# First batch of a softmax-weighted convolution before a max-out layer: softmax in two halves, half of the halo masked on GpSimd, and seven taps summed on TensorE for columns 8 to 11

## The chip, the cores and the metric

The kernel runs on one core of one Trainium2 chip. The metric is the device time of the slowest core (here the only one) in microseconds, as the median of several executions. The engines are TensorE (PE, with its weight load PEld), VectorE (DVE), ScalarE (ACT), GpSimd (POOL) and SyncE (SP, which here only issues transfers). An execution with the hardware profiler gives the trace from which all views below are taken.

## The reference, cut to what matters

```python
# x: [8, 4160, 192], weight_gen: [8, 4160, 8 heads, 7 taps], w1, w2: [192, 1024], w_out: [1024, 192]
w = exp(weight_gen - max over taps);  w = w / (sum over taps + 1e-9)
x_pad = six rows of zeros in front of each of the 8 sequences
y[b, s, h, g] = sum over k of w[b, s, h, k] * x_pad[b, s + k, h, g]      # 8 heads of 24 values
x1 = y.reshape(33280, 192)
out = maximum(x1 @ w1, x1 @ w2) @ w_out
```

A causal convolution with seven taps, whose weights are a softmax of their own for each row and head, is followed by a max-out layer.

## The kernel before

The 33280 rows are laid out as 128 partitions with 260 rows ("columns") each. Sixteen partitions hold one sequence, so the first partition of each sixteen needs six zero rows ahead of its first row, and the other partitions need the last six rows of their neighbour: this is the halo, which is loaded as `xs[:, 0:6*192]` and multiplied by a mask of 0 or 1. The columns are worked in batches of 16 (the last has 4). For a batch, `exp_sum` (ACT), `red` (DVE), `ln` (ACT) and `shift` (DVE) turn the raw weights into log-softmax values, `weights` (ACT) writes the exponentials doubled in bf16, `mul` (DVE) multiplies seven shifted copies of x with them, and `adds` (DVE) sums the taps.

```python
def exp_sum(b):
    e_ts[b] = pe_.tile([P, BATCHES[b][1] * WGC], FP32, name="e_t", tag="e")
    nc.scalar.activation(out=e_ts[b], in_=wg_ts[b], func=AF.Exp)

def red(b, i=0, of=1):
    ...
    nc.vector.reduce_sum(out=s_ts[b][:, hs], in_=_sub(e_ts[b], at, ap), axis=AX.X)

def ln(b):
    nc.scalar.activation(out=s_ts[b], in_=s_ts[b], func=AF.Ln)

def adds(b, o, first=False, beside=...):
    nc.vector.tensor_tensor(out=taps(0, 1, 3), in0=taps(0, 1, 3), in1=taps(3, 1, 3), op=ALU.add)
    if first:          # taps 3, 4, 5 are in taps 0, 1, 2 now; tap 6 is still alone
        return
    ...                # two more additions, the last into y_t
```

The first two batches are worked in pieces of four columns. For them `sum_transpose` adds the taps and transposes the result in one go on TensorE, by matrix products with an identity, and ACT copies the result to `yt`. With `LEFT` it reads four partial sums that a first addition on DVE has left, otherwise all seven taps. From batch 2 on DVE makes all three additions, and a transposing DMA gives `yt`.

```python
LEFT = (0, 1, 2, K - 1)

def sum_transpose(u, taps=range(K)):
    ...
    for k in range(6):
        for t in taps:
            for r in range(2):
                nc.tensor.matmul(yps[...], lhsT=m_t[half(r), at:at + P], rhs=ident[half(r), half(r)], ...)
    nc.scalar.copy(out=_sub(yt, ...), in_=_sub(yps, ...))
```

The maximum is taken as `x1 @ w1 + relu(x1 @ (w2 - w1))`: `wd` is `w2 - w1`, `hidden` multiplies `yt` with it on TensorE (two tiles for each group at first, three later) and applies the relu on ACT into `rd_t`, and `w10` is `w1 @ w_out`. `keep_warm` multiplies an identity with nothing to do. The engines work through their instructions in the order of the program text. The start of that text:

```python
load_wg(0, nc.sync)                      # weights of batch 0: one transfer
...                                      # halo, first four columns of x, first halves of w1 and w2
load_first(4)                            # columns 4 to 7 of x, into xs
...
exp_sum(0)
red(0)
ln(0)
shift(0)
nc.scalar.activation(out=xb_ts[0][:, 0:PAD * D], in_=xs[:, 0:PAD * D], func=AF.Copy, scale=msk[:, 0:1])
for o in (0, 4, 8, 12):
    weights(0, o)                        # two instructions each
nc.vector.tensor_copy(out=xb_ts[0][:, PAD * D:(PAD + 4) * D], in_=xs[:, PAD * D:(PAD + 4) * D])
mul(0, 0)
...
nc.scalar.copy(out=w1["E"][:, 0:HF], in_=ws["E", 0][:, 0:HF])
nc.scalar.copy(out=xb_ts[0][:, (PAD + 4) * D:(PAD + 8) * D], in_=xs[:, (PAD + 4) * D:])
...
nc.gpsimd.tensor_copy(out=gate[0:64, :], in_=ws["T", 1][:, 0:1])   # holds back GpSimd's own loads
load_x(0, 8, 4)
...
keep_warm(30)
w_diff(0, nc.scalar.copy)                # two subtractions on DVE, three copies on ACT
sum_transpose(0)
keep_warm(6)
mul(0, 4)
nc.scalar.copy(out=w1["E"][:, HF:F], in_=ws["E", 0][:, HF:F])
hidden(0)
nc.scalar.copy(out=w1["T"], in_=ws["T", 0])
w_diff(1, nc.vector.tensor_copy)
mul(0, 8)
sum_transpose(1)
exp_sum(1)
red(1)
adds(0, 8, True)
hidden(1)
ln(1)
shift(1)
mul(0, 12)
tp = w1_transposed()
hidden(2)
...
weights(1, 0)
mul(1, 0)
adds(1, 0, True)
sum_transpose(2, LEFT)
...
```

Of the kernel before, what the change touches and what calls it, by code (L numbers as in the profile page):

```python
# [9 lines left out]
FP32 = mybir.dt.float32  # L10
BF16 = mybir.dt.bfloat16
I32 = mybir.dt.int32
AF = mybir.ActivationFunctionType
ALU = mybir.AluOpType
# [3 lines left out]
def _sub(base: bass.AP, off: int, dims):  # L18
    ap = [list(base.ap[0])] + [[int(s), int(c)] for s, c in dims]
    return dataclasses.replace(base, offset=base.offset + off, ap=ap)  # L20
# [3 lines left out]
def kernel(  # L24
# [9 lines left out]
    nc = tc.nc  # L34

    B, S, D = x.shape
    H, K = weight_gen.shape[2], weight_gen.shape[3]
    F = moe_w1.shape[1]
    P = 128
    PAD = K - 1  # L40
    WGC = H * K
    FCH = F // P
    CPP = B * S // P
# [5 lines left out]
    BATCHES = [(c, min(16, CPP - c)) for c in range(0, CPP, 16)]  # L49
# [3 lines left out]
    def pieces(b):  # L53
        n = BATCHES[b][1]
        at, done = [], 0
        for w in (4, 4, 4, 4) if b < 2 else (8, 8) if n == 16 else (n,):
            at.append((done, w))
            done += w
        return at
# [17 lines left out]
    pe_ = ctx.enter_context(tc.tile_pool(name="pe", bufs=2))  # L77
# [20 lines left out]
    wg_ts, xb_ts, e_ts, s_ts, en_ts, y_ts, yt_ts = {}, {}, {}, {}, {}, {}, {}  # L98

    m_t = pm.tile([P, K * 16 * D], BF16, name="m_t")  # L100

    def load_wg(b, eng):
        c0, n = BATCHES[b]
        wg_ts[b] = pwg.tile([P, n * WGC], FP32, name="wg_t", tag="wg")
        eng.dma_start(
            out=wg_ts[b],
            in_=bass.AP(tensor=weight_gen.tensor, offset=c0 * WGC,
                        ap=[[CPP * WGC, P], [1, n * WGC]]),
        )

    def load_x(b, o, n):

# [9 lines left out]
                                in_=xb_ts[b - 1][:, 16 * D:(16 + PAD) * D])  # L122


    def exp_sum(b):
        e_ts[b] = pe_.tile([P, BATCHES[b][1] * WGC], FP32, name="e_t", tag="e")
        nc.scalar.activation(out=e_ts[b], in_=wg_ts[b], func=AF.Exp)  # L127

    def part(b, i, of):

        n = BATCHES[b][1]
        h0, h1 = n * i // of * H, n * (i + 1) // of * H
        return slice(h0, h1), h0 * K, [[K, h1 - h0], [1, K]]

    def red(b, i=0, of=1):
        if i == 0:
            s_ts[b] = psm.tile([P, BATCHES[b][1] * H], FP32, name="sum_t", tag="sum")
        hs, at, ap = part(b, i, of)
        nc.vector.reduce_sum(out=s_ts[b][:, hs], in_=_sub(e_ts[b], at, ap), axis=AX.X)  # L139

    def ln(b):
        nc.scalar.activation(out=s_ts[b], in_=s_ts[b], func=AF.Ln)  # L142

    def shift(b, i=0, of=1):
        hs, at, ap = part(b, i, of)
        w_t = _sub(wg_ts[b], at, ap)
        nc.vector.tensor_tensor(out=w_t, in0=w_t, in1=_sub(s_ts[b], hs.start, [[1, hs.stop - hs.start], [0, K]]),  # L147
                                op=ALU.subtract)
# [15 lines left out]
    def mul(b, o):  # L164

        n = dict(pieces(b))[o]
        if n == 4 and b < 2:
            m_out = _sub(m_t, K * o * D, [[64, 2], [P, K * 6], [1, 64]])
            x_in = _sub(xb_ts[b], o * D, [[2 * D, 2], [D, K], [1, 2 * D]])
        else:  # L170
            m_out = m_t[:, K * o * D:K * (o + n) * D]
            x_in = _sub(xb_ts[b], o * D, [[D, K], [1, n * D]])
        nc.vector.tensor_tensor(  # L173
            out=m_out, in0=x_in,
            in1=_sub(en_ts[b], o * WGC * 2, [[2, K * n * H], [0, G // 2], [1, 2]]),
            op=ALU.mult,
        )

    def adds(b, o, first=False, beside=lambda i, of: None):


        w = dict(pieces(b))[o]
        n = w * D

        def taps(at, step, cnt):
            return _sub(m_t, K * o * D + at * n, [[step * n, cnt], [1, w * D]])

        beside(0, 3)
        nc.vector.tensor_tensor(out=taps(0, 1, 3), in0=taps(0, 1, 3), in1=taps(3, 1, 3), op=ALU.add)  # L189
        if first:  # L190
            return
        beside(1, 3)
        if b not in y_ts:
            y_ts[b] = py.tile([P, 16 * D], BF16, name="y_t", tag="y")
        nc.vector.tensor_tensor(out=taps(0, 2, 2), in0=taps(0, 2, 2), in1=taps(1, 5, 2), op=ALU.add)  # L195
        beside(2, 3)

        nc.vector.tensor_tensor(  # L198
            out=_sub(y_ts[b], o * D, [[64, 2], [P, 3 * w // 2], [1, 64]]),
            in0=taps(0, 1, 1), in1=taps(2, 1, 1), op=ALU.add,  # L200
        )
# [22 lines left out]
    def half(j):  # L224
        return slice(64 * j, 64 * j + 64)


    LEFT = (0, 1, 2, K - 1)

    def sum_transpose(u, taps=range(K)):  # L230

        b, o, n = UNITS[u]
        assert n == 4
        yps = ps["r" if "r" in ps else "o"].tile([P, 1024], FP32, name="yps", tag="op")
# [3 lines that stand above are left out]
                    at = (K * o + t * n) * D + k * P  # L238
                    nc.tensor.matmul(
                        yps[:, r * 512 + k * 64:r * 512 + (k + 1) * 64],  # L240
                        lhsT=m_t[half(r), at:at + P], rhs=ident[half(r), half(r)],
                        start=(k == 0 and t == taps[0]), stop=(t == taps[-1]),
                        skip_group_check=True,
                    )
        yt = pyt.tile([P, 8 // 2 * 3 * P], BF16, name="yt", tag="yt")
        nc.scalar.copy(out=_sub(yt, 0, [[64, 2], [P, 6], [1, 64]]),  # L246
                       in_=_sub(yps, 0, [[512, 2], [64, 6], [1, 64]]))
        yt_ts[u] = yt
# [154 lines left out]
    for g in range(3, len(GROUPS)):  # L403
        most = 4 if g == 3 else 2 if GROUPS[g][1] == 2 or len(OUTS[-1]) == 4 else 4
        n = min(most, ready[g] - c)
# [78 lines left out]
    msk = consts.tile([P, 1], FP32, name="msk")  # L484
    gate = consts.tile([P, 1], FP32, name="gate")

    with tc.tile_pool(name="pstage", bufs=1) as pstage:
        ident_f = pstage.tile([P, P], FP32, name="ident_f")
        xs = pstage.tile([P, (PAD + 8) * D], FP32, name="xs")
        ws = {(kind, wi): pstage.tile([nr, F], FP32, name=f"ws{wi}{kind}")  # L490
              for kind, nr in (("E", P), ("T", 64)) for wi in range(2)}

        load_wg(0, nc.sync)
        nc.vector.memset(xs[0:1, 0:PAD * D], 0.0)
        for p0, p1, eng in ((16, P, nc.sync), (1, 16, nc.gpsimd)):
            eng.dma_start(
                out=xs[p0:p1, 0:PAD * D],
                in_=bass.AP(tensor=x.tensor, offset=(p0 * CPP - PAD) * D,
                            ap=[[CPP * D, p1 - p0], [1, PAD * D]]),
# [11 lines left out]
        def load_w(h):  # L511
            for kind, r0, nr in (("E", 0, P), ("T", P, 64)):
                for wi, wsrc in enumerate((moe_w1, moe_w2)):
# [14 lines left out]
        nc.vector.tensor_single_scalar(out=msk_i, in_=msk_i, scalar=1, op=ALU.min)  # L528
        nc.vector.tensor_copy(out=msk, in_=msk_i)
        nc.vector.tensor_copy(out=ident, in_=ident_f)  # L530
        exp_sum(0)
        red(0)
        ln(0)
        shift(0)
        xb_ts[0] = pxb.tile([P, (16 + PAD) * D], BF16, name="xb_t", tag="xb")
        nc.scalar.activation(out=xb_ts[0][:, 0:PAD * D], in_=xs[:, 0:PAD * D], func=AF.Copy,
                             scale=msk[:, 0:1])
        for o in (0, 4, 8, 12):
            weights(0, o)
        nc.vector.tensor_copy(out=xb_ts[0][:, PAD * D:(PAD + 4) * D],  # L540
                              in_=xs[:, PAD * D:(PAD + 4) * D])
        mul(0, 0)
        w1 = {kind: pstage.tile([nr, F], BF16, name="w1" + kind)
              for kind, nr in (("E", P), ("T", 64))}
# [3 lines left out]
        def w_diff(h, copy):  # L548

            c0, c1, c2 = (slice(s * F + h * HF, s * F + (h + 1) * HF) for s in range(3))  # L550
            nc.vector.tensor_tensor(out=wd[:, c0], in0=ws["E", 1][:, c0], in1=ws["E", 0][:, c0],
                                    op=ALU.subtract)
            copy(out=wd[64:P, c2], in_=wd[0:64, c0])
            copy(out=wd[0:64, c1], in_=wd[64:P, c0])
            nc.vector.tensor_tensor(out=wd[0:64, c2], in0=ws["T", 1][:, c0], in1=ws["T", 0][:, c0],
                                    op=ALU.subtract)
            copy(out=wd[64:P, c1], in_=wd[0:64, c2])
# [6 lines left out]
            out=wo[:, :].rearrange("p (f d) -> p f d", d=D),  # L564
            in_=bass.AP(tensor=moe_w_out.tensor, offset=0, ap=[[D, P], [P * D, FCH], [1, D]]),
# [23 lines left out]
        def keep_warm(times):  # L589

            for _ in range(times):
                nc.tensor.matmul(warm[:, 0:512], lhsT=ident, rhs=_sub(ident, 0, [[0, 4], [1, P]]),  # L592
                                 start=True, stop=True, skip_group_check=True)

        keep_warm(30)
        w_diff(0, nc.scalar.copy)
        sum_transpose(0)
        keep_warm(6)
        mul(0, 4)


        nc.scalar.copy(out=w1["E"][:, HF:F], in_=ws["E", 0][:, HF:F])
        hidden(0)
        nc.scalar.copy(out=w1["T"], in_=ws["T", 0])
        w_diff(1, nc.vector.tensor_copy)
        mul(0, 8)
        sum_transpose(1)
        exp_sum(1)
        red(1)
        adds(0, 8, True)  # L610
        hidden(1)
        ln(1)
        shift(1)
        mul(0, 12)
# [26 lines left out]
        weights(1, 0)  # L641
        mul(1, 0)
        adds(1, 0, True)
        sum_transpose(2, LEFT)
        load_x(2, 0, 16)
        load_wg(4, nc.gpsimd)
        rd = room(3)
# [138 lines left out]
```

The softmax here doesn't subtract the row's maximum and nothing guards it: scores larger than these inputs give would overflow.

## Time and profile before

| what | value |
|---|---|
| median of three runs | 413.91 us (413.67 to 413.95) |
| span of the profiled execution | 412.1 us |
| PE busy | 397.0 us, 96% |
| PEld busy | 316.0 us, 77% |
| DVE busy | 376.9 us, 91% |
| ACT busy | 359.2 us, 87% |
| POOL busy | 76.8 us, 19% |
| DMA | 65.68 MB, mean 159 GB/s |
| granted clock of TensorE | 0.997 |

A share of the span is an average over stages. The page also cuts the span into 40 equal slices of some 10.3 us each, with one digit of busy tenths for each engine, which shows the stages. The chain of waits follows the work that ended last back from the end, at each step to what released it. A timeline line gives the start in us, the duration in us, the engine, the line of the program, the operation and its operands, and in brackets how long the engine sat idle ahead of it and what ended that.

### The profile page before, as it was taken

How to read it: one execution, taken by the hardware profiler on the slowest of the kernel's cores; microseconds unless marked ns; L12 is line 12 of the kernel's file. 1: busy time of each engine (PE TensorE's matmuls, PEld its weight loads, DVE VectorE, ACT ScalarE, POOL GpSimd, SP SyncE). 2: the span in 40 equal slices, each digit the busy share in tenths (PEclk: the TensorE clock that was granted, in tenths of full speed). 3: DMA queues.
4: the chain of work that ended last, by engine and by line, in shares of the span. 5: the costliest groups of instructions: out<-in, count | busy, mean ns of one | idle time of the engine just before them, and what ended most of it. 6: DMA issues, size and time to landing. Idle time of an engine off the chain costs nothing.

```text
span 412.1 us, 15844 instructions
## 1 busy us (share of the span) xinstructions
PE 397.0 (96%) x7276; PEld 316.0 (77%) x7276; DVE 376.9 (91%) x218; ACT 359.2 (87%) x425; POOL 76.8 (19%) x102
## 2 busy tenths in 40 slices
PE   7879999999999999999999999999999999999994
PEld 2669899677777787777777777777777677777794
DVE  5999999999999999999999999999999999999000
ACT  5899998989999988999988999989998988888771
POOL 1510102212211212222012222220122221210000
PEclk9999999999999999999999999999999999999998
DMA  8975525775656875864896496578549747654613
GB/s 250 254 177 162 145 77 133 177 157 139 171 119 153 220 156 122 219 179 103 137 267 145 103 258 165 88 230 208 118 97 241 174 67 232 156 87 126 165 77 118
DMA packets 60242, 65.68 MB, mean 159 GB/s; under 512 B 47601, under 2 KB 48497, under 8 KB 60176
## 3 DMA queue, kind: packets, MB, share of 16 engines
q1 hardware_dynamic: 51904, 40.47, 35.4%
q0 software_dynamic: 8128, 24.11, 28.3%
q8 instruction: 57, 0.93, 0.9%
q10 hardware_dynamic: 144, 0.10, 0.1%
q14 instruction: 9, 0.07, 0.1%
HBM read 35.96 MB, written 25.56 MB: 149 GB/s over the span
## 4 chain that ended last, share of the span: by engine, by line
PE 44%; DVE 36%; ACT 12%; issue 3%; DMA 3%; SPq 1%; DVEq 0%; ACTq 0%
PE op_ps L315 21%; PE hd L275 19%; DVE m_t L173 18%; DVE m_t L189 8%; ACT rd_t L285 7%; DVE m_t L195 5%; PE op_ps L327 4%; DMA xs<-in_x_dram 2%; DVE y_t L198 2%; DVE sum_t L139 2%; DVE wg_t L147 1%; ACT en_t L158 1%; DMA yt<-y_t 1%; ACT yt L246 1%; PE hdp L275 1%
## 5 line engine op out<-in xcount | busy, mean ns | idle before, releaser
L285 ACT ACTIVATE rd_t<-hd 128x1024 bf16<-128x1024 f32 (+1 forms) x206 | 234.7, 1188 | 27.9 <-PE hd L275 26.4
L315 PE MATMUL op_ps<-wo,rd_t 64*128 64x192 bf16 x4160 | 210.5, 243 | 0.1
L315 PEld LDWEIGHTS <-rd_t 64*128 64x128 bf16 x4160 | 180.8, 94 | 15.7 <-ACTq L348 0.3
L275 PE MATMUL hd<-yt,wd 64*128 64x512 bf16 (+1 forms) x1584 | 187.5, 360 | 2.0 <-ACT rd_t L285 1.9
L173 DVE TENSOR_TENSOR m_t<-xb_t,en_t 128x10752 bf16<-128x10752 bf16 (+1 forms) x37 | 187.5, 5070 | 0.3 <-ACT en_t L158 0.3
L275 PEld LDWEIGHTS <-wd 64*128 64x128 bf16 x1776 | 94.0, 94 | 45.8 <-issue 4.9
L215 POOL CAST gate<-yt 128x1 f32<-128x1 bf16 x29 | 41.4, 1429 | 273.3 <-DMA yt<-y_t 273.3
L189 DVE TENSOR_TENSOR m_t<-m_t 128x4608 bf16<-128x4608 bf16 (+1 forms) x34 | 79.5, 2339 | 0.1
L371 ACT COPY o_t<-op_ps 128x384 f32<-128x384 f32 (+1 forms) x99 | 57.1, 588 | 13.7 <-PE op_ps L315 13.5
L327 PE MATMUL op_ps<-w,yt 64*128 64x192 bf16 x780 | 55.5, 243 | 1.7 <-ACT o_t L371 1.0
L327 PEld LDWEIGHTS <-yt 64*128 64x128 bf16 x780 | 38.4, 94 | 18.1 <-issue 2.6
L195 DVE TENSOR_TENSOR m_t<-m_t 128x3072 bf16<-128x3072 bf16 (+1 forms) x29 | 50.0, 1723 | 0.1
L158 ACT ACTIVATE en_t<-wg_t 128x896 bf16<-128x896 f32 (+2 forms) x45 | 35.3, 816 | 0.0
L198 DVE TENSOR_TENSOR y_t<-m_t 128x1536 bf16<-128x1536 bf16 (+1 forms) x29 | 27.3, 941 | 0.5
L361 DVE COPY o_t<-op_ps 128x192 f32<-128x192 f32 x1 | 0.4, 359 | 25.3 <-ACT o_t L361 25.3
L147 DVE TENSOR_TENSOR wg_t<-wg_t,sum_t 128x280 f32<-128x280 f32 (+4 forms) x45 | 22.0, 488 | 0.4 <-ACT sum_t L142 0.4
L139 DVE TENSOR_REDUCE sum_t<-e_t 128x64 f32<-128x448 f32 (+2 forms) x30 | 19.5, 650 | 2.5 <-ACT e_t L127 2.5
L115 POOL DMA_DIRECT2D xb_t<-in_x_dram x32 | 17.3, 540 | 23.1 <-DVE m_t L173 22.9
L127 ACT ACTIVATE e_t<-wg_t 128x896 f32<-128x896 f32 (+1 forms) x17 | 16.0, 939 | 2.5 <-DMA wg_t<-in_weight_gen_dram 2.5
L285 ACT ACTIVATE rd_t<-hdp 128x1024 bf16<-128x1024 f32 x16 | 15.9, 1027 | 1.0 <-PE hdp L275 1.0
L275 PE MATMUL hdp<-yt,wd 64*128 64x256 bf16 x192 | 13.0, 269 | 1.9 <-ACT rd_t L285 1.1
L592 PE MATMUL warm<-ident 128*128 128x512 bf16 x36 | 10.1, 445 | 3.0 <-DVE ident L530 3.0
(46 smaller groups left out, 74.4 us busy)
## 6 DMA issues: line engine op xcount, KB each, us to landing
out_dram<-o_t SPq DMA_DIRECT2D x28, 768.0 KB, 4.4
xb_t<-in_x_dram POOLq DMA_DIRECT2D x28, 384.0 KB, 4.8
wg_t<-in_weight_gen_dram POOLq DMA_DIRECT2D x14, 448.0 KB, 5.9
xb_t<-xb_t POOLq DMA_DIRECT2D x16, 288.0 KB, 5.0
out_dram<-o_t SPq DMA_DIRECT2D x8, 384.0 KB, 2.9
wg_t<-in_weight_gen_dram SPq DMA_DIRECT2D x2, 448.0 KB, 4.8
xs<-in_x_dram SPq DMA_DIRECT2D x2, 384.0 KB, 6.7
xb_t<-in_x_dram POOLq DMA_DIRECT2D x1, 768.0 KB, 6.9
```

The costliest lines, as they stand in the source:

```text
L139: nc.vector.reduce_sum(out=s_ts[b][:, hs], in_=_sub(e_ts[b], at, ap), axis=AX.X)
L158: nc.scalar.activation(out=_sub(en_ts[b], (o * WGC + j * N * K) * 2, [[2 * N, K], [2, N], [1, 2]]), in_=_sub(wg_ts[b], (o * H + j * N) * K ...
L173: nc.vector.tensor_tensor(out=m_out, in0=x_in, in1=_sub(en_ts[b], o * WGC * 2, [[2, K * n * H], [0, G // 2], [1, 2]]), op=ALU.mult,)
L189: nc.vector.tensor_tensor(out=taps(0, 1, 3), in0=taps(0, 1, 3), in1=taps(3, 1, 3), op=ALU.add)
L195: nc.vector.tensor_tensor(out=taps(0, 2, 2), in0=taps(0, 2, 2), in1=taps(1, 5, 2), op=ALU.add)
L198: nc.vector.tensor_tensor(out=_sub(y_ts[b], o * D, [[64, 2], [P, 3 * w // 2], [1, 64]]), in0=taps(0, 1, 1), in1=taps(2, 1, 1), op=ALU.add,)
L215: nc.gpsimd.tensor_copy(out=gate, in_=yt[:, 0:1])
L275: nc.tensor.matmul(hid_out(t, f, j), lhsT=wd[half(j), s * F + f * P:s * F + (f + 1) * P], rhs=_sub(yt_ts[u][half(j), :], (s + j) % 3 * P, ...
L285: nc.scalar.activation(out=rd[:, k * 1024:(k + n) * 1024], in_=hd[:, at:at + n * 1024], func=AF.Relu)
L315: return nc.tensor.matmul(op_out(c), lhsT=rd[half(r), k * 1024 + at:k * 1024 + at + P], rhs=wo[half(r), f * D:(f + 1) * D], start=False, s ...
L327: nc.tensor.matmul(op_out(c + j), lhsT=yt_ts[u][half(j), (3 * i + (s + j) % 3) * P:(3 * i + (s + j) % 3 + 1) * P], rhs=w10[half(j), s * D: ...
L371: nc.scalar.copy(out=_sub(o, c % 24 * D, [[D, len(qs)], [h * D, 2], [1, D]]), in_=_sub(tile_, at + (qs[0] - p) * D, [[D, len(qs)], [512, 2 ...
```

## The change

Three things are done, all in the first 30 us of the kernel. The softmax of batch 0 is split: its weights are loaded in two transfers of eight columns, and each of the four steps to the log-softmax becomes two instructions of half the size, so that ACT and DVE can work on different halves at one time. The first half of the halo (576 of 1152 values in each partition) is masked by GpSimd instead of ACT. For columns 8 to 11 of batch 0 the addition on DVE is taken away, and TensorE sums all seven taps. Along with this the idle products move (26 and 8 instead of 30 and 6), and the copy of the last 64 rows of w1 (`w1["T"]`) moves behind the copy of the second `yt` on ACT.

```diff
-    def load_wg(b, eng):
+    def load_wg(b, eng, of=1):
 ...
-        eng.dma_start(out=wg_ts[b], in_=..., ap=[[CPP * WGC, P], [1, n * WGC]])
+        w = n * WGC // of
+        for i in range(of):
+            eng.dma_start(out=wg_ts[b][:, i * w:(i + 1) * w], in_=..., ap=[[CPP * WGC, P], [1, w]])
 ...
-    def exp_sum(b):
-        e_ts[b] = pe_.tile([P, BATCHES[b][1] * WGC], FP32, name="e_t", tag="e")
-        nc.scalar.activation(out=e_ts[b], in_=wg_ts[b], func=AF.Exp)
+    def exp_sum(b, i=0, of=1):
+        if i == 0:
+            e_ts[b] = pe_.tile([P, BATCHES[b][1] * WGC], FP32, name="e_t", tag="e")
+        w = BATCHES[b][1] * WGC // of
+        nc.scalar.activation(out=e_ts[b][:, i * w:(i + 1) * w], in_=wg_ts[b][:, i * w:(i + 1) * w], func=AF.Exp)
 ...
-    def ln(b):
-        nc.scalar.activation(out=s_ts[b], in_=s_ts[b], func=AF.Ln)
+    def ln(b, i=0, of=1):
+        s_t = s_ts[b][:, part(b, i, of)[0]]
+        nc.scalar.activation(out=s_t, in_=s_t, func=AF.Ln)
 ...
-        load_wg(0, nc.sync)
+        load_wg(0, nc.sync, 2)
 ...
-        exp_sum(0)
-        red(0)
-        ln(0)
-        shift(0)
+        for step in (exp_sum, red, ln, shift):
+            for i in range(2):
+                step(0, i, 2)
         xb_ts[0] = pxb.tile([P, (16 + PAD) * D], BF16, name="xb_t", tag="xb")
-        nc.scalar.activation(out=xb_ts[0][:, 0:PAD * D], in_=xs[:, 0:PAD * D], func=AF.Copy,
+        HP = PAD * D // 2
+        nc.gpsimd.tensor_scalar(out=xb_ts[0][:, 0:HP], in0=xs[:, 0:HP], scalar1=msk[:, 0:1], scalar2=None,
+                                op0=ALU.mult)
+        nc.scalar.activation(out=xb_ts[0][:, HP:2 * HP], in_=xs[:, HP:2 * HP], func=AF.Copy,
                              scale=msk[:, 0:1])
 ...
-        keep_warm(30)
+        keep_warm(26)
         w_diff(0, nc.scalar.copy)
         sum_transpose(0)
-        keep_warm(6)
+        keep_warm(8)
 ...
-        nc.scalar.copy(out=w1["T"], in_=ws["T", 0])
         w_diff(1, nc.vector.tensor_copy)
         mul(0, 8)
         sum_transpose(1)
+        nc.scalar.copy(out=w1["T"], in_=ws["T", 0])
         exp_sum(1)
         red(1)
-        adds(0, 8, True)
         hidden(1)
 ...
-        sum_transpose(2, LEFT)
+        sum_transpose(2)
```

More of the change, by code (lines that the diff above doesn't have):

```diff
@@ L100 @@
     m_t = pm.tile([P, K * 16 * D], BF16, name="m_t")
-    def load_wg(b, eng):
+    def load_wg(b, eng, of=1):
         c0, n = BATCHES[b]
         wg_ts[b] = pwg.tile([P, n * WGC], FP32, name="wg_t", tag="wg")
[L105 to L109, printed above, removed]
+        w = n * WGC // of
+        for i in range(of):
+            eng.dma_start(
+                out=wg_ts[b][:, i * w:(i + 1) * w],
+                in_=bass.AP(tensor=weight_gen.tensor, offset=c0 * WGC + i * w,
+                            ap=[[CPP * WGC, P], [1, w]]),
+            )
     def load_x(b, o, n):
```

## The prediction

> **What bounds the kernel now.** I read the busy shares by slice first, then the chain of waits in order of time, then the timeline around every place where TensorE stood still, and last the first 25 us. The slices show that averages do not help: both PE and DVE are nearly full in every slice but the first and the last few.
>
> ```profile
> PE   7879999999999999999999999999999999999994
> ...
> DVE  5999999999999999999999999999999999999000
> ```
>
> DVE has no gap from slice 2 to slice 37 and then nothing to do; PE goes on for another 25 us. Which of them sets the pace is told by the chain of waits (start, duration, what):
>
> ```profile
> 136.04 1.32 PE op_ps L315 x32
> ...
> 144.67 1.32 PE op_ps L315 x32
> ...
> 212.46 5.75 DVE m_t L173
> ...
> 236.12 5.75 DVE m_t L173
> ...
> 342.83 4.00 DMA yt<-y_t
> 346.87 0.82 PE hd L275 x6
> ```
>
> Two rates can be read. PE repeats its pattern every 144.67 - 136.04 = 8.63 us for six columns, which is 23.02 us for a batch of 16. DVE repeats every 236.12 - 212.46 = 23.66 us. So DVE is slower by 0.64 us in each batch: it starts with a lead over PE and loses it. At 346.83 the last transfer of this chain (a transposed `y_t`) lands, and PE goes on with it at once; from there on PE alone sets the end. The timeline shows PE's weight load held until the very moment at which a `yt` lands, which the GpSimd copy `gate` marks:
>
> ```profile
> 311.09 0.33 PEld L275 LDWEIGHTS <-wd 64*128 64x128 bf16 x5 [0.20 <-issue]
> 311.17 1.75 POOL L215 CAST gate<-yt 128x1 f32<-128x1 bf16 x1 [9.10 <-DMA yt<-y_t]
> ...
> 323.54 1.01 PEld L275 LDWEIGHTS <-wd 64*128 64x128 bf16 x12 [1.00 <-PE op_ps L315]
> 323.55 1.18 POOL L215 CAST gate<-yt 128x1 f32<-128x1 bf16 x1 [9.63 <-DMA yt<-y_t]
> ...
> 346.87 0.33 PEld L275 LDWEIGHTS <-wd 64*128 64x128 bf16 x5 [0.43 <-issue]
> 346.95 1.44 POOL L215 CAST gate<-yt 128x1 f32<-128x1 bf16 x1 [9.37 <-DMA yt<-y_t]
> ```
>
> The idle names in the brackets mislead (no engine had just finished). The three stalls are 0.20 + 1.00 + 0.43 = about 1.6 us by the weight load, and about 1.4 us if I take PE's own gap of 0.81 at the second. This is all that DVE costs PE after 48 us. So the end is DVE's stream, through the `yt` of 346.83, plus PE's fixed rest. If DVE's stream moves earlier by d, the end moves by d, up to 1.4 us; there PE's own stream takes over.
>
> PE's own stream starts with ACT: from 11.70 to 31.5 us the chain is ACT almost without a break (it waits 0.40 us for PE at 16.18). The start:
>
> ```profile
> 11.70 0.83 ACT L547 CAST xb_t<-xs 128x768 bf16<-128x768 f32 x1 [0.63 <-DMA xs<-in_x_dram]
> ...
> 20.49 1.92 ACT L285 ACTIVATE rd_t<-hdp 128x1024 bf16<-128x1024 f32 x2
> 21.00 1.08 DVE L139 TENSOR_REDUCE sum_t<-e_t 128x128 f32<-128x896 f32 x1
> ...
> 22.00 1.35 DVE L189 TENSOR_TENSOR m_t<-m_t 128x2304 bf16<-128x2304 bf16 x1
> 22.30 0.31 ACT L142 ACTIVATE sum_t<-sum_t 128x128 f32<-128x128 f32 x1
> ...
> 23.27 1.08 DVE L147 TENSOR_TENSOR wg_t<-wg_t,sum_t 128x896 f32<-128x896 f32 x1
> ```
>
> ACT waits at 11.70 for columns 4 to 7 of x. Later, ACT's `ln` of batch 1 ends at 22.61, hidden behind DVE's addition at 22.00, the very one that the change removes.
>
> **What the Trainium skill says.** "SBUF — State Buffer", section "Who interferes with whom": a DVE instruction with two SBUF inputs or in a two-port mode and a GpSimd instruction that reads SBUF exclude one another for a whole instruction. The trace agrees: the GpSimd cast at 334.79, of one value per partition, takes 1.79 us and ends at 336.58, when DVE's product (330.79 + 5.75 = 336.54) ends. "GPSIMD Engine Reference", section "Elementwise — side-by-side cycle accounting": 1.8 cycles per element at 1.2 GHz in the best case; for 576 values that makes 0.86 us, an estimate, as no row here is such an operation. "DMA: Bandwidth & Descriptors", section "Queues, rings and completion order": on one DMA engine a ring is consumed in order. The trace fits: the x columns issued at 4.36 land only 7.32 us later, behind all that SyncE issued before them.
>
> **Part 1, the softmax in halves.** Before: exp 4.51 to 5.46, sum 5.50 to 6.58, ln to 6.92, subtraction to 8.05, then the exponentials from 8.08, because the mask (1.25 us) sits on ACT from 6.83; the product starts at 8.81. After: the DVE row for 128x448 takes 611 ns against 1081 for 128x896, so halving adds about 0.14 us per pair but overlaps. If the first half lands near 3.9 and the second near 4.6 (estimates from the landing at 4.51), the second exp ends near 5.2, the second sum near 5.8, the second ln near 6.1, and the subtractions near 7.1. But the halo lands at 1.27 + 5.5 = 6.8 and the first four columns of x at 1.66 + 6.0 = 7.7 (issue and time to landing of their transfers). DVE's cast of those columns then ends at 8.25, ACT's half mask (0.65 us, half of 1254 ns with its fixed part) at 7.45 and two exponentials near 8.1. The product could start at 8.3, 0.5 us earlier.
>
> **Part 2, the GpSimd mask.** It cannot start before the halo at 6.8 and finds the second subtraction holding the port until about 7.1; at 0.9 to 1.3 us it ends between 8.0 and 8.4. If it holds the port against the DVE cast at 7.7, the product starts at 8.6 to 9.0. So parts 1 and 2 together move it by between 0.5 us earlier and 0.2 us later.
>
> **Whether that is worth anything.** The next product needs ACT's cast of columns 4 to 7, which waits for the landing at 11.68 and ends at 12.53; it started at 12.89. So DVE can win at most 0.36 us here, and ACT nothing: its chain starts at 11.70 whatever happens before. The split makes 128 more packets. The queue view shows 188 packets of 0.68 MB at 95.1% of 16 engines from 3 to 5 us, or 162 ns for 3.6 KB, and 379 of 0.67 MB at 108.1% from 7 to 9 us, or 91 ns for 1.8 KB; a straight line leaves 23 ns for a packet, and 128 x 23 / 16 = 0.18 us. I call that **s**: the landing, and with it ACT's whole chain, slips by about 0.18 us.
>
> **Part 3, seven taps.** TensorE does 84 instead of 48 products there: before, 84 took 1.40 us and 48 took 0.87, so 0.53 us more. PE waits 0.39 us before them (until the addition ends) and 0.26 us later for ACT, so nothing reaches the chain. DVE loses one addition, 23.27 - 22.00 = 1.27 us. But `shift` then waits for `ln` of batch 1, which ends at 22.61 in ACT's own order, behind two relus. So `shift` starts at 22.65 + s instead of 23.27. The gain of DVE's stream is **d = 0.62 - s = 0.44 us**, whether or not part 1 won 0.36 us before: this wait swallows it. Moving the w1 copy behind the `yt` copy leaves ACT's sum as it was. After 23 us DVE waited for nothing; the exponentials that `mul(1, 0)` needs are ready at 26.41, and it would ask for them at 26.6 at the earliest, so d survives.
>
> **The sum.** 413.91 - 0.44 = 413.47 us, the end still set by DVE's stream.
>
> **Rivals.** (a) The naive sum: 1.27 us of addition and 0.36 us from part 1 move DVE by 1.6 us, PE takes over after 1.4 us, and the time is about 412.5. It needs an `ln` of batch 1 that is done by 21.9, and ACT's order speaks against that. (b) The start binds instead: the mask or the split holds ACT's or DVE's start back by 0.5 us or more; then d goes to zero, and PE's 1.4 us of slack hides the rest: 413.9 to 414.3. The 1.79 us cast is what speaks for it. (c) The landings decide: the transposes took 3.7 us as a rule but 4.3 at 319.17 and 4.0 at 342.83, when other transfers ran; shifted by half a microsecond they may meet others, 0.3 us either way.
>
> **Range and chances.** Point 413.45; (a) gives the lower end, 412.7, and (b) with (c) the upper, 414.2. Two per cent would be 8.3 us, while the whole stage in which the change works is 25 us with ACT full, so the chance of either side is about one in a hundred.
>
> **What would show it.** In the changed profile: DVE idle for 0.5 to 1.0 us before the subtraction of batch 1, released by ACT's `ln`; that subtraction near 22.7 to 22.9; the ACT cast of columns 4 to 7 near 11.9, still released by the DMA; the product of columns 0 to 3 between 8.3 and 9.0; the stalls at 311, 323 and 347 shrunk by about 0.4 us in sum, none gone everywhere. I am wrong if the subtraction starts before 22.3 (then rival a), if ACT's cast moves by more than 0.5 us (then the transfers were mis-sized), or if the chain no longer goes through DVE.

## The result, and the profile after

The changed kernel takes 416.50 us (median of 6 runs, 416.11 to 417.84), the kernel before 413.93 us (6 runs, 413.67 to 414.26). The ratio is 1.007 with a 95% interval of 1.0052 to 1.0088: within 2%, but slower, by about 2.6 us, and outside the predicted range.

The page of the changed kernel shows that another engine now sets the end. First three of the rows by slice, then the shares of the chain of waits by engine, after and before:

```profile
PE   7678899999999999999999999999999999999995
...
DVE  4989999999999999999999999999999999999100
...
PEclk9899999999999999999999999999999999999999
...
PE 83%; ACT 11%; issue 2%; DMA 2%; DVE 1%; POOL 0%; SPq 0%; POOLq 0%; DVEq 0%; ACTq 0%
```

```profile
PE 44%; DVE 36%; ACT 12%; issue 3%; DMA 3%; SPq 1%; DVEq 0%; ACTq 0%
```

DVE's third slice, which was full before, is at 8. PE's second, fourth and fifth slices have become emptier. The second slice of the granted clock has dropped below 9 tenths. The chain no longer goes through DVE (1%): it comes out of ACT (11%) and is then PE's own stream (83%). The timeline of the first 27 us shows why (SPq marks SyncE's issue of a transfer). First two lines of before, then after:

```profile
3.73 0.59 SPq L514 DMA_DIRECT2D ws1T<-in_moe_w_dram  x1
4.36 0.59 SPq L503 DMA_DIRECT2D xs<-in_x_dram  x1
```

```profile
3.33 1.12 ACT L131 ACTIVATE e_t<-wg_t 128x448 f32<-128x448 f32 x2 [1.33 <-DMA wg_t<-in_weight_gen_dram]
...
4.86 1.38 SPq L519 DMA_DIRECT2D ws1T<-in_moe_w_dram  x1
...
6.28 0.59 SPq L508 DMA_DIRECT2D xs<-in_x_dram  x1
...
8.87 0.78 ACT L543 ACTIVATE xb_t<-xs,msk 128x576 bf16<-128x576 f32 x1 [3.47 <-DMA xs<-in_x_dram]
8.99 1.99 POOL L541 TENSOR_SCALAR xb_t<-xs,msk 128x576 bf16<-128x576 f32 x1 [6.29 <-DMA xs<-in_x_dram]
...
11.01 2.96 DVE L178 TENSOR_TENSOR m_t<-xb_t,en_t 128x5376 bf16<-128x5376 bf16 x1 [0.55 <-POOL xb_t L541]
...
14.03 2.42 PE L244 MATMUL yps<-ident,m_t 64*128 64x64 bf16 x84 [3.46 <-DVE m_t L178]
...
14.61 0.83 ACT L554 CAST xb_t<-xs 128x768 bf16<-128x768 f32 x1 [2.10 <-DMA xs<-in_x_dram]
...
22.11 0.80 ACT L251 CAST yt<-yps 128x768 bf16<-128x768 f32 x1 [0.86 <-PE yps L244]
...
26.74 1.09 DVE L152 TENSOR_TENSOR wg_t<-wg_t,sum_t 128x896 f32<-128x896 f32 x1 [0.93 <-ACT sum_t L147]
```

The weights do what they were meant to do: the first exponential starts at 3.33 instead of 4.51. But what SyncE loads behind them is late. The halo lets ACT's mask start at 8.87, after 3.47 us of waiting; the first columns of x come at 9.9 instead of some 7.7. Columns 4 to 7 are issued at 6.28 instead of 4.36 and let ACT's cast start at 14.61 instead of 11.70. From there ACT's whole order of work is 2.9 us late. TensorE has run out of idle products and stands still for 3.46 us ahead of 14.03; its 84 products then take 2.42 us, where they took 1.40.

How the start becomes the end can be read from three lines of each kernel: the first `hidden` group of TensorE with the tiles of the steady state, TensorE's last products, and the last store that SyncE issues. First before, then after, then the version that loads the weights in one transfer (one_load below):

```profile
49.06 1.49 PE L275 MATMUL hd<-yt,wd 64*128 64x256 bf16 x24 [0.20 <-ACT rd_t L285]
...
404.56 2.16 PE L315 MATMUL op_ps<-wo,rd_t 64*128 64x192 bf16 x48
...
407.67 0.46 SPq L362 DMA_DIRECT2D out_dram<-o_t  x1
```

```profile
53.79 1.49 PE L280 MATMUL hd<-yt,wd 64*128 64x256 bf16 x24 [0.19 <-ACT rd_t L290]
...
408.16 2.16 PE L320 MATMUL op_ps<-wo,rd_t 64*128 64x192 bf16 x48
...
411.15 0.34 SPq L367 DMA_DIRECT2D out_dram<-o_t  x1
```

```profile
49.69 1.49 PE L280 MATMUL hd<-yt,wd 64*128 64x256 bf16 x24 [0.19 <-ACT rd_t L290]
...
404.02 2.16 PE L320 MATMUL op_ps<-wo,rd_t 64*128 64x192 bf16 x48
...
407.01 0.34 SPq L367 DMA_DIRECT2D out_dram<-o_t  x1
```

From the first of these lines to the end of TensorE's last product it is 357.7 us before, and 356.5 us in the two others: the stalls on DVE, 1.1 to 1.2 us, are gone. From that product to the end of the span it is 5.4 us before (412.1 - 406.7) and 4.5 us in the two others (414.8 - 410.3, 410.7 - 406.2): the last store leaves and lands 0.9 us sooner. So the changed kernel starts this stream 4.7 us later, saves 1.1 us of stalls and 0.9 us behind the last product, and ends 2.7 us later. The saving behind the last product stands in the traces of all seven versions that sum seven taps (4.5 to 4.6 us), and in none of those that keep the addition (4.8 to 5.8 us); why it goes with the seven taps was not found.

The 4.7 us are made up of four parts. ACT's cast of columns 4 to 7 is 2.9 us late. From the cast to the first relu ACT takes 0.2 us more (19.30 - 14.61 against 16.18 - 11.70), as the slow products and the eight idle products hold PE back. From that relu to the exponential of batch 1 it takes 1.0 us more, which is the wait of 0.86 us ahead of the second `yt` and what comes with it. The rest, 0.6 us, lies between that exponential and 53.79; one_load has it too (30.3 us against 29.4 before) and taps_only, with the seven taps alone, hardly (29.6), so it comes from another part of the change; which one was not isolated.

### The profile page after: what moved, and what is told of

It reads as the page before. It is cut to its first block, busy times and chain, and to the rows that moved or that the text cites. A ratio compares the mean times of both kernels' runs of the same rounds, so it can differ in the third digit from the quotient of the medians.

```text
span 414.8 us, 15920 instructions
## 1 busy us (share of the span) xinstructions
PE 398.0 (96%) x7310; PEld 317.5 (77%) x7310; DVE 376.1 (91%) x219; ACT 358.9 (87%) x427; POOL 81.4 (20%) x103
## 4 chain that ended last, share of the span: by engine, by line
PE 83%; ACT 11%; issue 2%; DMA 2%; DVE 1%; POOL 0%; SPq 0%; POOLq 0%; DVEq 0%; ACTq 0%
PE op_ps L320 38%; PE hd L280 36%; PE op_ps L332 7%; ACT rd_t L290 6%; DMA xs<-in_x_dram 2%; ACT en_t L163 1%; PE yps L244 1%; PE hdp L280 1%; ACT o_t L376 1%; DVE m_t L178 1%; ACT e_t L131 1%; PE warm L599 0%; POOL xb_t L541 0%; ACT yt L251 0%; ACT w1t L646 0%
## 5 line engine op out<-in xcount | busy, mean ns | idle before, releaser
L220 POOL CAST gate<-yt 128x1 f32<-128x1 bf16 x29 | 44.4, 1531 | 269.7 <-DMA yt<-y_t 269.7
L194 DVE TENSOR_TENSOR m_t<-m_t 128x4608 bf16<-128x4608 bf16 (+1 forms) x33 | 78.2, 2369 | 0.1
L376 ACT COPY o_t<-op_ps 128x384 f32<-128x384 f32 (+1 forms) x99 | 57.3, 592 | 13.5 <-PE op_ps L320 13.3
L152 DVE TENSOR_TENSOR wg_t<-wg_t,sum_t 128x280 f32<-128x280 f32 (+5 forms) x46 | 22.1, 481 | 0.9 <-ACT sum_t L147 0.9
L131 ACT ACTIVATE e_t<-wg_t 128x896 f32<-128x896 f32 (+2 forms) x18 | 16.1, 898 | 1.3 <-DMA wg_t<-in_weight_gen_dram 1.3
L244 PE MATMUL yps<-ident,m_t 64*128 64x64 bf16 x528 | 10.4, 198 | 4.2 <-DVE m_t L178 3.5
```

The source lines that it names most:

```text
L220: nc.gpsimd.tensor_copy(out=gate, in_=yt[:, 0:1])
L376: nc.scalar.copy(out=_sub(o, c % 24 * D, [[D, len(qs)], [h * D, 2], [1, D]]), in_=_sub(tile_, at + (qs[0] - p) * D, [[D, len(qs)], [512, 2 ...
```

## The experiments

My theory after the result was that the second weights transfer is the cause: it stands ahead of the halo and of x in SyncE's queue, and what follows is late. Rivals were the mask on GpSimd, the new order of ACT, the smaller packets of the split load, and an advantage of the addition that could be absent. Later two forms of the theory were to be told apart: that what follows is merely issued later, or that one more transfer in the queue costs by itself. The texts of expectation were written before each run and carry their own names for these. "Cast" is always ACT's cast of columns 4 to 7.

### The parts alone

**split_only**: the kernel before, with the weights of batch 0 loaded in two transfers and nothing else changed.

```diff
-    def load_wg(b, eng):
+    def load_wg(b, eng, of=1):
 ...
-        load_wg(0, nc.sync)
+        load_wg(0, nc.sync, 2)
```

> The kernel before with the load of batch 0's weights in two transfers, and nothing else changed. Theory A (the second transfer slows SyncE's whole stream of transfers; in the changed kernel columns 4 to 7 of x land at about 14.6 us instead of 11.7): the ACT cast of those columns starts near 14.6, DVE's stream is late by about 2.6 us and the time is 416.2 to 416.8 us. Theory B (the GpSimd mask, 1.99 us there, holds everything up): the cast stays near 11.9 and the time is 413.8 to 414.2 us. Theory C (the order of the w1T copy and the idle products cost it): 413.8 to 414.2 us as well.

Measured: 417.08 us (7 runs) against 413.95, ratio 1.0061 (1.0037 to 1.0086). Two lines of its timeline:

```profile
4.30 1.55 SPq L516 DMA_DIRECT2D ws1T<-in_moe_w_dram  x1
...
15.43 0.83 ACT L549 CAST xb_t<-xs 128x768 bf16<-128x768 f32 x1 [2.64 <-DMA xs<-in_x_dram]
```

The split alone makes the whole loss: the cast is at 15.43, and SyncE needs 1.55 us for an issue (`ws1T`) that took 0.59.

**one_load**: the changed kernel, with the weights in one transfer again; the softmax is still worked in halves.

```diff
-        load_wg(0, nc.sync, 2)
+        load_wg(0, nc.sync)
```

> The changed kernel with batch 0's weights in one transfer again; the four steps of the softmax stay in halves, the GpSimd mask, the seven taps and the orders stay. Theory A: the columns land near 11.7 us again and the time is 412.9 to 413.6 us, the gain of the removed addition. Theory B and C: still 415.5 us or more.

Measured: 413.07 us (20 runs), ratio 0.998 (0.9972 to 0.9988). It is faster than both kernels. Its timeline:

```profile
4.32 0.58 SPq L508 DMA_DIRECT2D xs<-in_x_dram  x1
...
11.08 0.83 ACT L554 CAST xb_t<-xs 128x768 bf16<-128x768 f32 x1 [0.78 <-DMA xs<-in_x_dram]
...
22.43 1.09 DVE L152 TENSOR_TENSOR wg_t<-wg_t,sum_t 128x896 f32<-128x896 f32 x1 [0.47 <-ACT sum_t L147]
```

One argument removes the loss. The cast is even earlier than before (11.08 against 11.70). DVE is no longer in the chain of waits (0%, PE 82%): with the stalls gone, TensorE's own stream sets the end.

**taps_only**: the kernel before, with part 3 alone.

```diff
-        adds(0, 8, True)
 ...
-        sum_transpose(2, LEFT)
+        sum_transpose(2)
```

> The kernel before with only the addition of columns 8 to 11 taken from DVE and all seven taps summed on TensorE. By the prediction's third part: batch 1's subtraction starts near 22.65 instead of 23.27 us, after a wait for ACT's ln, and the time is 413.2 to 413.4 us (0.6 us less). If the removed addition counted in full and the wait were absent, 412.5 to 412.8 us.

Measured: 413.15 us (9 runs), ratio 0.9976 (0.9963 to 0.9988). The line that the prediction was about:

```profile
22.37 1.09 DVE L147 TENSOR_TENSOR wg_t<-wg_t,sum_t 128x896 f32<-128x896 f32 x1 [0.40 <-ACT sum_t L142]
```

The subtraction of batch 1 starts at 22.37 instead of 23.27, and DVE waits 0.40 us for ACT's `ln`. As taps_only and one_load cannot be told apart, the halved softmax, GpSimd's mask, the moved idle products and the moved copy brought nothing that was measured: the whole gain goes with the seven taps. How much of it comes through DVE's stream is not shown, as 0.8 us of this trace's gain lie behind TensorE's last product (4.6 us to the end instead of 5.4).

**act_mask**: the changed kernel, with the whole halo masked by ACT.

```diff
-        nc.gpsimd.tensor_scalar(out=xb_ts[0][:, 0:HP], in0=xs[:, 0:HP], scalar1=msk[:, 0:1], ...)
-        nc.scalar.activation(out=xb_ts[0][:, HP:2 * HP], in_=xs[:, HP:2 * HP], func=AF.Copy,
+        nc.scalar.activation(out=xb_ts[0][:, 0:2 * HP], in_=xs[:, 0:2 * HP], func=AF.Copy,
                              scale=msk[:, 0:1])
```

> The changed kernel with the whole halo masked by ACT again, in one instruction. Theory A: the columns still land near 14.6 us and the time stays at 416.0 to 416.8 us. Theory B: the time falls to 413.0 to 413.8 us. Theory C: unchanged, 416 to 417 us.

Measured: 416.80 us (4 runs), ratio 1.0065 (1.004 to 1.0091); cast at 15.15. GpSimd's mask is slow, but it is not the cause.

### What of the second transfer costs

**act_queue**: the kernel before, with the second half of the weights issued by ACT at the same time, ahead of its table load.

```diff
-    nc.scalar.preload_act_table_set("natural_log_exp_and_others")
 ...
-        load_wg(0, nc.sync)
+        for h, eng in ((0, nc.sync), (1, nc.scalar)):
+            eng.dma_start(out=wg_ts[0][:, h * 8 * WGC:(h + 1) * 8 * WGC], in_=...)
+        nc.scalar.preload_act_table_set("natural_log_exp_and_others")
```

> The kernel before with batch 0's weights in two transfers of eight columns, the second issued by ACT ahead of its table load, so that SyncE issues the halo as early as before. Theory P: the packets are as small as in the changed kernel, the cast near 14 us, 416 us or more. Theory N: the cast at 11.4 to 12.0 us, 413.6 to 414.2 us.

Measured: 413.75 us (12 runs) against 413.88, ratio 0.9997 (0.9988 to 1.0005).

```profile
4.33 0.95 ACT L126 ACTIVATE e_t<-wg_t 128x896 f32<-128x896 f32 x1 [1.87 <-DMA wg_t<-in_weight_gen_dram]
...
11.14 0.83 ACT L553 CAST xb_t<-xs 128x768 bf16<-128x768 f32 x1 [0.25 <-DMA xs<-in_x_dram]
```

Two transfers are harmless if the second isn't in SyncE's queue. The Trainium skill says in "DMA: Bandwidth & Descriptors", section "Issuing engines are not separate DMA queues", that starting transfers from several engines saves only the issue time, as all run on the same 16 DMA engines. For the weights the trace agrees: they are complete no more than 0.2 us earlier (4.33 against 4.51). For what stands behind them the runs differ from it: the issue that SyncE saves is 0.46 us (the halo at 1.19, against 1.65 with both halves in its own queue in split_only), but the time differs by 0.64% (ratios 0.9997 and 1.0061), some 2.6 us.

**small_packets**: the kernel before, with one transfer of 256 packets of 1792 bytes. Columns 8 to 15 are computed with other weights than the reference's.

```diff
-        load_wg(0, nc.sync)
+        nc.sync.dma_start(out=_sub(wg_ts[0], 0, [[8 * WGC, 2], [1, 8 * WGC]]),
+            in_=bass.AP(..., ap=[[CPP * WGC, P], [16 * WGC, 2], [1, 8 * WGC]]))
```

> The kernel before with batch 0's weights in one transfer that reads two separate stretches of 1792 bytes for each partition (columns 0 to 7 and, instead of 8 to 15, 16 to 23; so columns 8 to 15 of the output are computed with other weights, with the same work): 256 packets of half the size, but one transfer. Theory P: the cast near 14.5 us, 416 to 417.5 us. Theory N: the cast at 11.4 to 12.0 us, 413.7 to 414.3 us.

Measured: 414.05 us (12 runs), ratio 1.0003 (0.9995 to 1.0012), cast at 11.08. The 128 more packets cost nothing.

**by_rows**: the kernel before, with two transfers of 64 partitions each; the packets keep their 3584 bytes.

```diff
-        load_wg(0, nc.sync)
+        wg_ts[0] = pwg.tile([P, 16 * WGC], FP32, name="wg_t", tag="wg")
+        for p0 in (0, 64):
+            nc.sync.dma_start(out=wg_ts[0][p0:p0 + 64, :], in_=...)
```

> The kernel before with batch 0's weights in two transfers on SyncE's queue, split by partitions (0 to 63, 64 to 127) and not by columns: 128 packets of 3584 bytes as before, but two transfers. Theory P (the packets of half the size do the harm): the cast of columns 4 to 7 on ACT starts at 11.4 to 11.9 us as before, 413.7 to 414.2 us. Theory N (one more transfer in SyncE's queue does it: it puts off the issue of the halo by 0.46 us, the transfer engines run dry and do not recover their rate): the cast near 14.5 to 15.5 us, 416 to 417.5 us.

Measured: 415.31 us (12 runs), ratio 1.0031 (1.0021 to 1.004); cast at 13.47. That lies between the two forecasts. So two transfers in one queue cost without small packets too, about half as much. Here the two issues alone take 1.21 us (0.87 with the split by columns).

**tiny_between**: the kernel before, with a transfer of one row of 224 bytes between the weights and the halo.

```diff
         load_wg(0, nc.sync)
+        tiny = pstage.tile([1, WGC], FP32, name="tiny")
+        nc.sync.dma_start(out=tiny, in_=...)
```

> The kernel before with one more transfer of a single row of 224 bytes (not used by anything) in SyncE's queue between the weights of batch 0 and the halo: the issue of the halo is put off by some 0.4 us and hardly a byte is added. Theory P: the cast at 11.4 to 12.1 us, 413.7 to 414.3 us. Theory N: the cast at 13.5 us or later, 415.5 to 417.5 us.

Measured: 414.75 us (20 runs, 412.93 to 417.54), ratio 1.0023 (1.0008 to 1.0037); cast at 12.55, again between the forecasts. A transfer that moves almost nothing costs 0.9 us (0.3 to 1.5 by the interval), and in the slowest executions 3 us and more.

**delay_only**: the kernel before; the halo's issue is made to wait for a small fill on DVE, with no transfer added.

```diff
+        hold = pstage.tile([1, 400], FP32, name="hold")
+        held_by = nc.vector.memset(hold, 0.0)
 ...
+            tc.add_manual_dep(halo.ins, held_by.ins.name, ...)   # SyncE's part of the halo
```

> The kernel before with the issue of the halo (and so of all that SyncE issues after it) put off until a small memset on DVE has ended, near 1.6 to 1.65 us instead of 1.19: as late as in the changed kernel, with no transfer more. Theory T (the later issue is what does the harm): the ACT cast of columns 4 to 7 at 13.5 us or later, 415.3 to 417.3 us. Theory X (one more transfer in the queue does it by itself): the cast at 11.4 to 12.2 us, 413.7 to 414.3 us.

Measured: 414.08 us (12 runs), ratio 1.0004 (0.9995 to 1.0012). The dose failed: the fill ended early, and the halo was issued at 1.30, only 0.11 us later than before (1.19). The run decides nothing.

**delay_half** and **delay_one**: the same with a longer fill and with a wait for the fill of `xs`; the halo is issued at 1.72 and at 2.08.

```diff
+        hold = pstage.tile([1, 800], FP32, name="hold")      # delay_half: twice the length
+        held_by = nc.vector.memset(hold, 0.0)
 ...
+        held_by = nc.vector.memset(xs[0:1, 0:PAD * D], 0.0)  # delay_one
```

> The kernel before with the issue of the halo put off until a memset of 800 values on DVE has ended, near 1.7 us instead of 1.19 (in the changed kernel 1.65); no transfer more. Theory T (the later issue does the harm): the ACT cast of columns 4 to 7 at 13.5 us or later, 415.3 to 417.3 us. Theory X (the additional transfer does it by itself): the cast at 11.4 to 12.2 us, 413.8 to 414.5 us.

> The kernel before with the issue of the halo put off until DVE's memset of the halo's first row has ended, near 2.1 us, 0.9 us later than before. Theory T: the cast at 14 us or later, 416 us or more. Theory X: every landing moves by at most the delay, the cast at 11.8 to 12.6 us, 413.8 to 415.0 us.

Measured: delay_half 415.18 us (19 runs, 413.76 to 418.27), ratio 1.003 (1.0014 to 1.0045); the profiled execution ran at a lower clock (424.14 us) and is left out, and of its trace only the time of the halo's issue is used. delay_one 414.96 us (7 runs), ratio 1.0022 (1.001 to 1.0034); cast at 12.27. A later issue alone costs 0.9 to 1.2 us, and the longer delay does not cost more. So in the median lateness is a part of the loss, but not the 2.6 us. The spread says more than the median: the kernel before stays within 413.14 and 414.94 us on the same chip, while delay_half reaches 417.5 to 418.3 us in three of its executions, as much as split_only. So a later issue alone can, in some executions, cost as much as the second transfer.

**tiny_first**: the kernel before, with the tiny transfer ahead of the weights.

```diff
+        tiny = pstage.tile([1, WGC], FP32, name="tiny")
+        nc.sync.dma_start(out=tiny, in_=...)
         load_wg(0, nc.sync)
```

> The kernel before with the additional transfer of one row of 224 bytes as the first of SyncE's queue, ahead of the weights. If the number of transfers counts: as with the tiny one behind the weights (cast 12.55, 414.75 us), 414.4 to 415.1 us. If it counts only between the weights and the halo: the cast at 11.4 to 12.2 us, 413.8 to 414.4 us.

Measured: 414.48 us (12 runs), ratio 1.0009 (1.0 to 1.0018); cast at 11.61, for which ACT did not wait. Everything is issued 0.4 us later, and it costs no more than that. The interval overlaps that of tiny_between (1.0008 to 1.0037), so that the place matters for so small a transfer is probable and not shown.

**after_late_half**: the changed kernel, with the second half of the weights on SyncE, but issued behind the halo.

```diff
-        load_wg(0, nc.sync, 2)
+        def load_half(h):
 ...
+        load_half(0)
 ...                                 # the halo
+        load_half(1)
```

> The changed kernel with both halves of the weights on SyncE's queue, but the second one issued behind the halo. If the harm comes from a second transfer of weights ahead of the halo: the cast at 11.2 to 12.3 us and 412.9 to 414.0 us. If any additional transfer of this size in this part of the queue does it: the cast at 13.5 us or later, 415.3 us or more.

Measured: 414.34 us (12 runs), ratio 1.0005 (0.9995 to 1.0015); cast at 12.62. By the ratios, each against the kernel before on the same chip, this is 0.25% above one_load; with the second half ahead of the halo it is 0.9% (1.007 against 0.998). So the transfer costs much less behind the halo, and is still not free: cast and time lie between the two forecasts.

What the runs have in common is easiest to see if the path to the cast is cut in two: when SyncE issues columns 4 to 7, and how long it is from there to the cast. All values are from the timelines, one execution each; only runs in which ACT really waited for the transfer are listed. The execution of after_w1t_first (below) is the slowest of its 20.

| kernel | issue, us | cast, us | issue to cast, us |
|---|---|---|---|
| before | 4.36 | 11.70 | 7.3 |
| taps_only | 4.37 | 11.37 | 7.0 |
| one_load | 4.32 | 11.08 | 6.8 |
| act_queue | 4.33 | 11.14 | 6.8 |
| small_packets | 4.46 | 11.08 | 6.6 |
| after_act_queue | 4.55 | 11.41 | 6.9 |
| tiny_between | 4.58 | 12.55 | 8.0 |
| after_late_half | 5.07 | 12.62 | 7.6 |
| delay_one | 5.28 | 12.27 | 7.0 |
| by_rows | 6.45 | 13.47 | 7.0 |
| split_only | 5.90 | 15.43 | 9.5 |
| act_mask | 5.88 | 15.15 | 9.3 |
| after_w1t_first | 5.54 | 15.67 | 10.1 |
| after | 6.28 | 14.61 | 8.3 |

The loss has two parts. In the changed kernel the issue is 1.9 us later: 0.47 us for the additional issue, and the rest because SyncE's two issues of `ws0T` and `ws1T` take 1.28 and 1.38 us instead of 0.56 and 0.59. And the way from the issue to the landing is about 1 us longer, in split_only 2.2; with one execution each, how much of that difference is chance is open. by_rows has only the first part, tiny_between almost only the second. The stretches of the trace show the second part as a rate: us, length, busy time of five engines, granted clock, DMA share, GB/s. First before, then after, then delay_one:

```profile
3.00:6.00 3.00, 2.99 (x8) 1.07 (x9) 0.51 (x1) 0.95 (x1) 0.00 (x0) 1.00 1.03 310
6.00:9.00 3.00, 3.00 (x13) 1.31 (x12) 2.33 (x4) 2.39 (x6) 0.00 (x0) 1.00 1.04 334
9.00:12.00 3.00, 2.77 (x25) 1.16 (x24) 3.00 (x2) 2.37 (x8) 1.01 (x2) 1.00 1.03 330
```

```profile
3.00:6.00 3.00, 2.98 (x8) 1.03 (x9) 2.06 (x4) 1.64 (x4) 0.00 (x0) 1.00 0.91 230
6.00:9.00 3.00, 3.00 (x14) 1.35 (x13) 0.18 (x1) 0.13 (x1) 0.01 (x1) 1.00 1.01 269
9.00:12.00 3.00, 1.57 (x8) 0.48 (x5) 1.55 (x2) 3.00 (x10) 1.98 (x1) 1.00 1.06 227
12.00:15.00 3.00, 0.97 (x38) 0.98 (x40) 3.00 (x3) 0.90 (x2) 1.52 (x3) 0.74 1.06 266
```

```profile
9.00:12.00 3.00, 3.00 (x15) 1.18 (x12) 2.70 (x2) 2.81 (x9) 0.47 (x1) 1.00 1.04 261
```

The DMA share adds up the times that packets took, over 16 engines. From 6 to 12 us it is 1.01 to 1.06 in both kernels, but after the change 269 and 227 GB/s are moved instead of 334 and 330, although the small packets of the weights have long landed. It is not a matter of larger or smaller packets either. From 9 to 12 us the trace has

```profile
DMA packets 480, 0.99 MB, mean 330 GB/s; under 512 B 55, under 2 KB 55, under 8 KB 480
```

before and

```profile
DMA packets 343, 0.68 MB, mean 227 GB/s; under 512 B 51, under 2 KB 51, under 8 KB 343
```

after: of the same mean size (2.1 and 2.0 KB), but a packet takes 149 ns instead of 103 (the share times 16 engines times 3 us, by the number of packets). Why a second transfer at 1.2 us makes packets slower until 12 us stays open. Packet size does not explain it (small_packets), and lateness explains at most a part: delay_one, with no transfer more, has 261 GB/s from 9 to 12 us.

### Two steps of the changed kernel on their own

**after_act_queue**: the changed kernel, with the second half of the weights issued by ACT.

```diff
-    nc.scalar.preload_act_table_set("natural_log_exp_and_others")
 ...
-        load_wg(0, nc.sync, 2)
+        for h, eng in ((0, nc.sync), (1, nc.scalar)):
+            eng.dma_start(out=wg_ts[0][:, h * 8 * WGC:(h + 1) * 8 * WGC], in_=...)
+        nc.scalar.preload_act_table_set("natural_log_exp_and_others")
```

> The changed kernel with the second half of batch 0's weights issued by ACT ahead of its table load, instead of by SyncE; all else of the change stays. If only the place of that transfer in SyncE's queue costs the time: the cast at 11.0 to 11.8 us, 412.8 to 413.5 us, like the changed kernel with one transfer (413.07). If a second transfer costs wherever it is issued: 415.5 us or more.

Measured: 413.41 us (14 runs) against 414.12, ratio 0.9986 (0.9977 to 0.9994); cast at 11.41. The loss is gone again, with two transfers and all of the rest in place. But ACT's first exponential starts at 4.29: on two queues the halves come together, so the softmax in halves has nothing to win.

**after_w1t_first**: the changed kernel, with the copy of `w1["T"]` at its old place ahead of the second `yt`.

```diff
         hidden(0)
+        nc.scalar.copy(out=w1["T"], in_=ws["T", 0])
 ...
         sum_transpose(1)
-        nc.scalar.copy(out=w1["T"], in_=ws["T", 0])
```

> The changed kernel with the copy of w1's last 64 rows on ACT ahead of the second yt copy again, as in the kernel before. In the changed kernel's trace ACT stood 0.86 us for TensorE's sums ahead of that yt copy, which this copy (1.04 us) would fill: 415.5 to 416.0 us. If the wait is not on the path: 416.3 to 416.7 us, as the changed kernel.

Measured: 415.75 us (20 runs, 414.34 to 418.48), ratio 1.0041 (1.0028 to 1.0055), against 1.007 (1.0052 to 1.0088) for the changed kernel. That fits with the 0.86 us of ACT's wait, which the copy would fill; but the intervals overlap a little and the executions spread over 4 us, so it is probable and not shown.

## Why the prediction was wrong

- **What bounds the kernel.** DVE's stream was in the chain of the kernel before (36%), and the stalls on it are 1.1 to 1.2 us, somewhat below the estimate of 1.4. That the end would be "still set by DVE's stream" held only in part, though: in taps_only DVE is still in the chain (31%), but in one_load, where the start stays in place, the stalls are gone, and PE's stream sets the end.
- **The step that failed: s.** The prediction gave the split 128 packets at 23 ns on 16 engines, 0.18 us, and concluded that ACT's chain "slips by about 0.18 us". It slipped by 2.9. The form of the term was wrong, not only its size: small_packets shows that the packets cost nothing, while the transfer, of which the sum had no term, costs the later issue and the lower rate of what follows. The landings of the halo (6.8) and of the first columns (7.7) were taken over from before as well; they came at 8.8 and 9.9.
- **Part 1.** The halves of the weights landed at 3.3 and by 3.9, 0.6 us and more ahead of the estimates (3.9 and 4.6). That was worth nothing, because the product then waited for the halo. The sentence that ACT's chain "starts at 11.70 whatever happens before" named the right instruction and the wrong reason for calm: it is a landing, and the change touches the queue that it is in.
- **Part 2.** GpSimd's mask took 1.99 us (1.73 to 1.86 in the other versions that have it) instead of 0.9 to 1.3. The estimate of 0.86 us from "GPSIMD Engine Reference", section "Elementwise — side-by-side cycle accounting", was a best case for another operation; the measurement decides. The mask released the first product (0.55 us of DVE's wait), as the prediction feared, and this is not what the end depends on (act_mask). That the mask would hold the port against DVE's cast was not seen: the cast ran from 9.90 to 10.46, inside the mask (8.99 to 10.98), and took 0.56 us against 0.55 before; in one_load it took 0.75.
- **Part 3.** Right for the start of the subtraction: it waits for ACT's `ln`, 0.40 us in taps_only and 0.47 in one_load, and starts at 22.37 and 22.43 instead of the 22.65 that the prediction gave without s. In taps_only ACT's first relu was 0.26 us earlier than before (15.92 against 16.18), as the columns had landed earlier; without that, the 0.90 us are 0.64, and 0.62 were forecast. That the time fell by 0.80 us (0.5 to 1.5 by the interval) fits, but in part by luck: the 0.8 us behind the last product were in no term of the sum.
- **The moved copy.** "Leaves ACT's sum as it was" holds only while ACT finds its work ready. In the late start it waits 0.86 us for PE, and the copy that could have filled this comes after.
- **The rivals.** (b), a late start that takes over, was the right one and was made too small: 0.5 us from the mask or the split, covered by PE's slack. With 4.7 us it was beyond any slack. Two of the three signs named for being wrong were met: the cast moved by more than 0.5 us, and the chain left DVE.
- **Not foreseen.** The idle products ended at 10.57, with the sums ready only at 14.03. The Trainium skill, "TensorE: Matmul & The Clock Gate", section "Part 1: The HAM clock gate", has the clock go down to half after an idle window of about 3.4 us. The trace agrees only in part. The clock does fall to half, for some 3 us, and the 84 products take 1 us more, but it falls at about 13.5 us, 2.9 us after the last idle product; in split_only it falls at 14.5 us, with only 2.05 us without products ahead of the 84 products, which had begun by then (after, then split_only; in the lines of stretches the clock stands third from the end):

```profile
13.50:14.00 0.50, 0.00 (x0) 0.00 (x0) 0.50 (x2) 0.00 (x0) 0.50 (x2) 0.50 1.15 312
```

```profile
13.98 2.04 PE L241 MATMUL yps<-ident,m_t 64*128 64x64 bf16 x84 [2.05 <-DVE m_t L175]
...
14.50:15.00 0.50, 0.50 (x31) 0.50 (x24) 0.50 (x2) 0.00 (x0) 0.50 (x2) 0.50 1.29 177
```

The prediction put no price on the four idle products that were taken away.

## What to carry to other kernels

In this start, in which the loads fill the DMA engines, a load cut in two in one queue made what stands behind it 2.9 us later, where its packets had been priced at 0.18 us. So first look which landing the chain starts from, and keep that transfer's place in the queue. If an early piece of data is wanted, try the second piece on another engine's queue (nothing lost here) or behind what the chain needs (0.25% above one transfer here), and ask beforehand whether the consumer of the early piece isn't waiting for something else. Where a start hangs on landings, look at the spread of the executions and not only at the median. The seven taps were worth all that this change had to give, and they needed two of its lines.

## What the runs showed of the hardware

- One more small transfer in a loaded queue: 224 bytes between two large loads cost 0.9 us of the kernel's time (tiny_between, 1.0008 to 1.0037), ahead of both 0.4 us (tiny_first, 1.0 to 1.0018).
- SyncE's issues are not of fixed length: `ws0T` and `ws1T` took 0.56 and 0.59 us before, 1.28 and 1.38 us after, and up to 1.55 us in split_only.
- A DMA share of 1.06 is no measure of what is moved: 227 GB/s at 1.06 after, 330 GB/s at 1.03 before, from 9 to 12 us and with packets of the same mean size (149 ns each against 103).
- GpSimd took 1.73 to 1.99 us for 576 values in each partition, multiplied by one value per partition, from f32 to bf16.
- TensorE's clock fell to half (0.50 from 14.5 us) in split_only, although only 2.05 us ahead of that had been without products.
